# ReLU-squared attention and mixture of depths on one core: heads in a ring of five units instead of three batches

## The chip, the core and the metric

The kernel runs on one core of a Trainium2 chip. The time is that of one execution on the device, in microseconds (us). The core has five instruction queues that run side by side and wait for one another by semaphores: PE (TensorE, matmuls; its weight loads are shown as PEld), ACT (ScalarE), DVE (VectorE), POOL (GpSimd) and SP (SyncE). POOL and SP compute next to nothing here: they start DMAs.

## The reference

Two steps, cut to what is computed. B is 8, H is 12, S is 448, D of a head is 64; the rows of x have 768 elements, F is 1024, and 128 rows of each batch are chosen.

```python
scores = scale * np.matmul(q, k.transpose(0, 1, 3, 2))
attn = np.maximum(scores, 0.0) ** 2 / S
attn_out = np.matmul(attn, v)
x = attn_out.transpose(0, 2, 1, 3).reshape(B, S, H * D)
...
scores = np.einsum('bsd,d->bs', x, w_gate)
out = x.copy()
for b in range(B):
    top_idx = np.argpartition(-scores[b], capacity)[:capacity]
    xe = x[b, top_idx]
    h = np.maximum(xe @ w1, 0.0)
    ye = h @ w2
    g = 1.0 / (1.0 + np.exp(-scores[b, top_idx]))
    out[b, top_idx] = x[b, top_idx] + g[:, None] * ye
```

All inputs and the output are float32 in HBM; on the chip heads, weights and rows are bfloat16, and POOL's DMAs convert while they load.

## The kernel before

**Units.** Four heads make a unit: a batch has NU = 3 units, the kernel 24, numbered u = 3 b + i. A batch of the output ("row" in the words of the change) is 448 rows of x.

**The order is written out.** The string ORDER is a list of some 1200 items; a loop at the end of the kernel calls one function for each, in this order, and nothing reorders them later. Each engine thus gets its own instructions in the order of the list and works through them one after the other; where the data of one comes from another engine, it waits there. The functions, with u a unit, c one of seven chunks of 64 keys, b a batch:

- `L,n,b,i0,i1` (L94) starts on POOL the load of one unit of q, k or v: 224 KB as bfloat16, v in three DMAs. `W` loads a piece of w1 or w2 (256 or 192 KB), 14 in all. The program gives POOL's DMAs eight semaphores in turn, so that a DMA isn't started before the one eight places ahead of it has landed.
- `T,u,n,at` transposes a unit's q or k on PE: 28 matmuls of 64x64 and as many weight loads, 56 instructions. `TE` copies both out of PSUM to qkt on DVE (L185).
- `S,u,c,at`: scores of one chunk, four matmuls of 448 columns (L220). `R,u,c,eng`: ReLU of the scores out of PSUM to r_sb, on ACT (A, L181) or DVE (D, L183). There are 168 S and 168 R, and R is a handy counter of how far the list is: "at R 28" is behind 28 R. `Q,u,c0,c1`: square of four or three chunks in place on DVE (L232).
- `V,u,c,n`: squares times v, four matmuls (L242). `X`: the result, scaled, to xT_sb (L181 or L187), which holds x transposed.
- `XR,u,at` and `XE,u,eng`: x back to rows by eight transposing matmuls on PE (L262) and a copy by ACT or DVE. `XB,u`: the same by two transposing DMAs from SP (L280). Units 0 to 8 (rows 0 to 2) go by XR and XE, 9 to 23 by XB.
- `ST,b,j` stores a quarter of the rows from POOL (L286).
- The second step, for a batch b: `g`, `bc`, `col`, `colE` make the scores of the gate in rows and columns; `rk` (DVE, L330), `cs`, `rank` and `hot` rank them and make a selection matrix; `sel`, `sE` make the indices; `xe`, `xeE` gather by matmul; `h` and `hE`, `y` and `yE` are the two layers; `gs`, `sig` the gate; `ADD` adds the result onto the stored rows by an indirect DMA from POOL (L468). The last batch has forms of its own (`xeh`, `hq`, `yq`, `xs`, `yS`), whose ADD writes whole rows. In the list these stand among the items of later units.

**Buffers.** PSUM is four places of two banks, "pair0" to "pair3", named by the argument `at`; every matmul result goes to one of them, and a place is free again when its result has been read. The heads lie in three buffers for each of q, k and v, one for a batch of three units (NBUF, L61); batch b uses buffer b % 3. qt_pool (transposed heads) and r_pool (scores and squares) have three buffers each, a buffer for a unit.

**The start.** q and k of unit 0 come by SP into float32 staging tiles (`Z,l`) and are converted by ACT and DVE (`Z,q0` to `Z,k1`); the identity for transposes is made by DVE and POOL (`Z,i`), and POOL's constants by `Z,t`, `Zi`.

Of the kernel before, what the change touches and what calls it, by code (L numbers as in the profile page):

```python
# [20 lines left out]
def kernel(  # L21
# [170 lines left out]
    def T(u, n, at):  # L192
# [3 lines left out]
        s_ = sb[n][b % NBUF]  # L196
        for jj in range(NC):
            c = CJ[jj] if n == "q" else jj
            o = S * "qk".index(n) + jj * 64
            for w in range(2):  # L200
                for g in range(2):
                    rows = slice(64 * g, 64 * g + 64)
                    nc.tensor.matmul(  # L203
                        out=t_ps[u][64 * w:64 * w + 64, g, o:o + 64],
                        lhsT=s_[rows, 2 * i + w, c * Dh:c * Dh + Dh], rhs=ident[rows, rows],
                        is_transpose=True, start=(jj == 0 and n == "q"), stop=(jj == NC - 1),
                        skip_group_check=True)
# [272 lines left out]
    R,1,5,A Zi,1 Q,0,4,7,D S,2,2,1 S,2,3,0 L,q,2,2,4 R,2,2,A S,3,0,2 L,k,4,0,2 R,2,3,A Q,1,0,4,D S,2,0,1 V,0,4,3  # L480
    W,2,7 V,0,5,4 V,0,6,5 R,2,0,A V,0,0,6 S,3,2,0 L,v,1,0,2 X,0,A S,3,3,1 R,3,2,D R,3,3,A S,3,5,3 L,q,1,4,6 Zt,0
    V,1,1,0,0 R,3,0,A Q,1,4,7,D V,1,2,1 V,1,3,2 Zi,2 S,3,4,1 L,k,2,2,4 R,3,5,A S,3,1,2 L,q,3,4,6 R,3,4,D R,3,1,A
    V,1,4,3 S,2,1,3 V,1,5,4 L,k,3,0,2 V,1,6,5 R,2,1,A V,1,0,6 Q,3,0,4,D T,4,q,2 S,2,4,1 L,q,3,2,4 T,4,k,2 X,1,A
    S,2,5,3 R,2,4,A L,v,0,4,6 S,2,6,0 TE,4,b,D R,2,6,A S,3,6,1 Q,2,0,4,D R,2,5,A S,4,5,2 L,q,2,0,2 S,4,4,0 R,3,6,A
    L,k,3,2,4 T,5,q,3 T,5,k,3 R,4,4,A S,4,2,1 TE,5,b,D W,1,5 R,4,2,A V,3,1,0,0 V,3,2,1 Q,3,4,7,D V,3,3,2 L,q,4,4,6
    S,4,6,3 R,4,5,A T,7,q,1 T,7,k,1 R,4,6,A W,1,4 S,4,1,2 Q,2,4,7,D V,3,4,3 V,3,5,4 R,4,1,A V,3,6,5 V,3,0,6
    S,4,0,3 L,v,1,2,4 X,3,A V,2,1,0,2 Q,4,4,7,D V,2,2,1 V,2,3,2 V,2,4,3 R,4,0,A V,2,5,4 S,4,3,0 V,2,6,5 L,q,3,0,2
    V,2,0,6 R,4,3,A TE,7,b,D S,5,4,3 L,k,2,4,6 R,5,4,A T,6,q,0 Q,4,0,4,D S,5,5,1 T,6,k,0 X,2,A L,q,4,0,2 S,5,1,3
    R,5,5,A S,5,3,2 L,k,5,2,4 Zt,1 R,5,1,A TE,6,b,D S,5,0,1 Zi,3 R,5,0,A S,5,6,3 W,1,1 R,5,3,D S,6,3,0 R,5,6,A
# [10 lines left out]
    rk,1,1 V,7,3,2 S,8,5,2 TE,10,b,D V,7,4,3 V,7,5,4 R,8,5,A V,7,6,5 V,7,0,6 L,q,5,2,4 sel,0,1 rk,1,2 X,7,A  # L500
    S,10,0,3 S,10,3,2 sE,0,0 Q,8,0,4,D ST,0,2 xe,0,0 xe,0,4 R,10,0,A xe,0,5 xe,0,2 xe,0,3 R,10,3,A XR,7,0
    L,q,5,0,2 xe,0,1 sE,0,1 XR,6,3 XE,7,D xeE,0,2,A W,2,2 T,11,q,2 XE,6,D S,9,0,0 T,11,k,2 S,10,5,1 R,9,0,A rk,1,0
    ST,1,3 h,0,0,3 h,0,2 TE,11,b,D R,10,5,A h,0,1 gs,0,0 L,v,3,0,2 h,0,5 sig,0 Q,8,4,7,D S,9,5,2 S,10,6,0 S,10,4,1
    R,9,5,A h,0,6 h,0,3 L,k,6,4,6 R,10,4,A rk,1,3 h,0,7 cs,1,2 ST,1,2 h,0,4 R,10,6,A rank,1 hot,1 S,9,2,2
    V,8,1,0,1 ST,0,3 V,8,2,1 hE,0,2,D R,9,2,A V,8,3,2 S,9,4,0 V,8,4,3 V,8,5,4 V,8,6,5 R,9,4,A ST,1,0 V,8,0,6
    Q,10,4,7,D S,10,2,2 L,q,6,2,4 y,0,0,0,3 y,0,1,0 X,8,A y,0,0,1 y,0,1,1 y,0,0,3 y,0,1,3 R,10,2,A sel,1,0
    L,v,3,4,6 y,0,0,4 y,0,1,4 Q,9,4,7,D XR,8,1 y,0,0,7 y,0,1,7 XE,8,A y,0,0,5 y,0,1,5 y,0,0,6 y,0,1,6 sE,1,0
    sE,1,1 Q,9,0,4,D L,k,5,0,2 xe,1,4 y,0,0,2 y,0,1,2 xe,1,1 ST,2,1 yE,0,2,A xe,1,5 xe,1,2 L,q,4,2,4 xe,1,0 xe,1,3
    T,12,q,3 xeE,1,2,A L,k,4,2,4 S,11,3,1 T,12,k,3 V,9,1,0,2 R,11,3,A V,9,2,1 TE,12,b,D V,9,3,2 L,q,7,0,2 S,10,1,0
# [110 lines left out]
```

## Time and profile before

| | |
|---|---|
| median of 3 runs | 223.0 us (221.33 to 227.87) |
| profiled execution | 221.9 us |
| its span, first to last instruction | 220.0 us |
| PE, DVE, ACT, POOL busy | 179.7, 171.0, 164.9, 114.2 us |
| HBM read, written | 39.32 MB, 14.16 MB |

The profile is of one execution. A row of the groups has the line, the engine, the operation, result and operands with their shapes, the count; then busy time in us, mean ns of one, and behind the second bar the idle time of the engine in front of them with what ended it. In the table of waits a row says who waited for whom: us in total, times, longest. "issue" is time in which an engine waited for nothing that the profile shows. In the timeline a row has start and length in us, and in brackets the idle time ahead of it. A busy PE isn't a PE at its peak: matmuls are pipelined and their ends are modelled. Busy times of one instruction reach over the start of the next, so the sum of means is above the busy time.

### The profile page before, as it was taken

The page shows a single profiled execution, that of the slowest core. Times are in us where ns is not written, and L with a number is a line of the kernel's source. Part 1 is how long each engine was busy: PE and PEld are TensorE (multiplying, and loading weights), DVE is VectorE, ACT ScalarE, POOL GpSimd, SP SyncE. Part 2 cuts the span into 40 slices and gives each one's busy share as a digit, 9 for nine tenths or more (in the row PEclk, how much of TensorE's full clock was granted, in tenths as well). Part 3 has the DMA queues.
Part 4 walks back from the last instruction along what each step waited for, and adds up shares of the span by engine and source line. Part 5 has one row for each costly group of instructions (what it writes and reads, how often), then busy time and mean ns, then how long its engine had stood idle before and what let it go on. Part 6 is the DMA issues. An engine that isn't in the chain of part 4 may idle for free. (4 is left out here: it accounts for less than half of the span.)

```text
span 220.0 us, 8241 instructions
## 1 busy us (share of the span) xinstructions
PE 179.7 (82%) x3689; PEld 117.9 (54%) x3689; DVE 171.0 (78%) x235; ACT 164.9 (75%) x210; POOL 114.2 (52%) x192
## 2 busy tenths in 40 slices
...
GB/s 182 136 179 145 197 200 204 201 203 199 205 235 216 240 292 202 176 242 239 122 179 166 201 231 191 322 176 114 108 153 221 5 48 51 277 153 106 234 98 0
DMA packets 42383, 38.75 MB, mean 176 GB/s; under 512 B 19110, under 2 KB 38572, under 8 KB 42348
## 3 DMA queue, kind: packets, MB, share of 16 engines
q0 software_dynamic: 25472, 33.37, 83.8%
q1 hardware_dynamic: 16876, 4.86, 18.3%
q8 instruction: 29, 0.48, 0.9%
...
HBM read 39.32 MB, written 14.16 MB: 243 GB/s over the span
## 5 line engine op out<-in xcount | busy, mean ns | idle before, releaser
L181 ACT ACTIVATE r_sb<-s_ps 128x896 bf16<-128x896 f32 x146 | 125.3, 937 | 15.8 <-PE s_ps L220 15.5
L232 DVE TENSOR_TENSOR r_sb<-r_sb 128x3584 bf16<-128x3584 bf16 (+1 forms) x48 | 84.9, 1783 | 3.1 <-ACT r_sb L181 2.7
L220 PE MATMUL s_ps<-qkt 64*64 64x448 bf16 x672 | 60.5, 379 | 14.0 <-ACT r_sb L181 5.2
L242 PE MATMUL o_ps<-r_sb,v_sb 64*64 64x448 bf16 x672 | 46.2, 371 | 4.0 <-issue 3.0
L220 PEld LDWEIGHTS <-qkt 64*64 64x64 bf16 x672 | 23.5, 109 | 34.2 <-issue 25.9
L286 POOL DMA_DIRECT2D out_dram<-x_sb x32 | 18.4, 636 | 45.1 <-DMA x_sb<-xT_sb 35.9
L242 PEld LDWEIGHTS <-v_sb 64*64 64x64 bf16 x672 | 23.0, 112 | 15.7 <-issue 6.6
L102 POOL DMA_DIRECT2D v_sb<-in_v_dram x48 | 28.2, 659 | 6.1 <-DMA k_sb<-in_k_dram 2.9
L183 DVE TENSOR_SCALAR r_sb<-s_ps 128x896 bf16<-128x896 f32 x22 | 23.8, 1087 | 7.8 <-PE s_ps L220 7.1
L185 DVE COPY qkt<-t_ps 128x1792 bf16<-128x1792 bf16 x24 | 25.9, 1084 | 3.3 <-PE t_ps L203 3.3
L291 PE MATMUL y_ps<-w_sb,hT 128*128 128x384 bf16 x128 | 25.6, 327 | 0.5 <-ACT g__4297 L375 0.5
L291 PE MATMUL h_ps<-xeT,w_sb 128*128 128x128 bf16 x384 | 25.5, 222 | 0.2 <-ACT xeT L181 0.2
L468 POOL DMA_INDIRECT out_dram<-gye,idx x8 | 14.3, 1783 | 20.6 <-ACT gye L181 6.6
L291 PEld LDWEIGHTS <-w_sb 128*128 128x128 bf16 x384 | 22.2, 99 | 4.7 <-issue 4.3
L181 ACT ACTIVATE xT_sb<-o_ps 128x896 bf16<-128x896 f32 (+1 forms) x20 | 18.3, 917 | 6.6 <-PE s_ps L220 3.7
...
L100 POOL DMA_DIRECT2D v_sb<-in_v_dram x24 | 16.4, 685 | 4.0 <-DMA k_sb<-in_k_dram 3.6
L203 PE MATMUL t_ps<-ident,q_sb 64*64 64x64 bf16 x672 | 10.6, 198 | 8.9 <-POOL ident L127 5.3
L291 PEld LDWEIGHTS <-hT 128*128 128x128 bf16 x128 | 10.6, 97 | 8.6 <-issue 2.6
L203 PEld LDWEIGHTS <-q_sb 64*64 64x64 bf16 x672 | 9.2, 111 | 11.0 <-ACT q_sb L181 4.8
L330 DVE SCALAR_TENSOR_TENSOR mask<-bc_sb,cols,tie 128x320 bf16<-128x320 f32 (+3 forms) x32 | 14.1, 481 | 0.3
...
## 6 DMA issues: line engine op xcount, KB each, us to landing
...
```

What stands on the lines that cost most here:

```text
L97: nc.gpsimd.dma_start(out=t[:, i0:i1], in_=head_src(n, b, i0, i1))
L100: nc.gpsimd.dma_start(out=t[:, i0:i1:2], in_=s_[:, 0::2])
L102: nc.gpsimd.dma_start(out=t[64 * h:64 * h + 64, i0 + 1:i1:2], in_=s_[64 - 64 * h:128 - 64 * h, 1::2])
L181: nc.scalar.activation(out=out_, in_=in_, func=func or AF.Copy, scale=scale)
L183: nc.vector.tensor_scalar(out=out_, in0=in_, scalar1=0.0, scalar2=None, op0=ALU.max)
L185: nc.vector.tensor_copy(out=out_, in_=in_)
L203: nc.tensor.matmul(out=t_ps[u][64 * w:64 * w + 64, g, o:o + 64], lhsT=s_[rows, 2 * i + w, c * Dh:c * Dh + Dh], rhs=ident[rows, rows], is_t ...
L220: nc.tensor.matmul(out=s_ps[u, c][64 * (g ^ w):64 * (g ^ w) + 64, w, :S], lhsT=qkt[u][rows, g, S + c * 64:S + c * 64 + 64], rhs=qkt[u][row ...
L232: (nc.gpsimd if eng == "P" else nc.vector).tensor_tensor(out=a, in0=a, in1=a, op=ALU.mult)
L242: nc.tensor.matmul(out=o_[64 * g:64 * g + 64, w, :S], lhsT=sb["v"][b % NBUF][rows, 2 * i + w, c * Dh:c * Dh + Dh], rhs=r_sb[u][rows, c, w, ...
L286: nc.gpsimd.dma_start(out=out[b].rearrange("(p c) d -> p c d", c=NC)[:, 4 * g + k0:4 * g + k0 + n], in_=x_rows[b][64 * g:64 * g + 64, k0:k ...
L291: nc.tensor.matmul(out=out_, lhsT=lhsT, rhs=rhs, start=start, stop=stop, skip_group_check=True, **kw)
```

## The change

The heads lie in a ring of NR = 5 buffers for each of q, k and v, one for a unit: unit u uses buffer u % 5. So a load of unit u writes what T (q, k) or V (v) of unit u - 5 has read, and the program waits for that. qt_pool and r_pool get a fourth buffer. Units 9 to 14 (rows 3 and 4) go by XR and XE instead of XB. The list is a new one: the same work in another order, with some evacuations moved between ACT and DVE (R 142 on ACT and 26 on DVE instead of 146 and 22; X 22 and 3 instead of 20 and 5, XE 6 and 9 instead of 2 and 7).

```diff
-    qt_pool = ctx.enter_context(tc.tile_pool(name="qt", bufs=3))
-    r_pool = ctx.enter_context(tc.tile_pool(name="r", bufs=3))
+    qt_pool = ctx.enter_context(tc.tile_pool(name="qt", bufs=4))
+    r_pool = ctx.enter_context(tc.tile_pool(name="r", bufs=4))
...
-    NBUF = 3
-    sb = {n: [const.tile([128, HH, NC * Dh], BF16, name=f"{n}_sb{i}") for i in range(NBUF)]
+    NR = 5
+    sb = {n: [const.tile([128, 2, NC * Dh], BF16, name=f"{n}_sb{i}") for i in range(NR)]
           for n in "qkv"}
...
     def L(n, b, i0, i1):
-        t = sb[n][b % NBUF]
+        t = sb[n][(b * NU + i0 // 2) % NR]
+        s_ = head_src(n, b, i0, i1)
         if n != "v":
-            nc.gpsimd.dma_start(out=t[:, i0:i1], in_=head_src(n, b, i0, i1))
+            nc.gpsimd.dma_start(out=t, in_=s_)
             return
-        s_ = head_src(n, b, i0, i1)
-        nc.gpsimd.dma_start(out=t[:, i0:i1:2], in_=s_[:, 0::2])
+        nc.gpsimd.dma_start(out=t[:, 0], in_=s_[:, 0])
         for h in range(2):
-            nc.gpsimd.dma_start(out=t[64 * h:64 * h + 64, i0 + 1:i1:2],
-                                in_=s_[64 - 64 * h:128 - 64 * h, 1::2])
+            nc.gpsimd.dma_start(out=t[64 * h:64 * h + 64, 1],
+                                in_=s_[64 - 64 * h:128 - 64 * h, 1])
...
-        s_ = sb[n][b % NBUF]
+        s_ = sb[n][u % NR]
...
-                        lhsT=s_[rows, 2 * i + w, c * Dh:c * Dh + Dh], rhs=ident[rows, rows],
+                        lhsT=s_[rows, w, c * Dh:c * Dh + Dh], rhs=ident[rows, rows],
...
-                                 lhsT=sb["v"][b % NBUF][rows, 2 * i + w, c * Dh:c * Dh + Dh],
+                                 lhsT=sb["v"][u % NR][rows, w, c * Dh:c * Dh + Dh],
...
     ORDER = """
-    Z,l Z,f Z,x Z,t L,q,0,2,4 Z,q0 Z,q1 Z,s Z,i L,k,0,2,4 T,0,q,0 Z,k0 Z,k1 L,k,0,4,6 Z,w T,0,k,0 Zg,1 L,k,1,0,2
+    Z,l Z,f Z,x L,q,0,2,4 L,k,0,2,4 L,q,0,4,6 Z,t Z,q0 Z,q1 Zi,0 Z,s Z,i Zt,0 Zi,1 Z,k0 Z,k1 T,0,q,0 Zi,2 Z,w Zt,1
```

The list as the engines get it is seen at three places. First SP, from its first load to its last transposing DMA, before:

```order
L123 DMA qf_100<-in_q_dram 128x2x448
L123 DMA kf_101<-in_k_dram 128x2x448
L124 DMA wgr_102<-in_moe_w_gate_dram 6x128
L280 DMA_TRANSPOSE x_sb_2178<-xT_sb0_94 128x4x128 x6
L280 DMA_TRANSPOSE x_sb_2853<-xT_sb1_95 128x4x128 x6
L280 DMA_TRANSPOSE x_sb_3461<-xT_sb2_96 128x4x128 x6
L280 DMA_TRANSPOSE x_sb_3978<-xT_sb0_94 128x4x128 x6
L280 DMA_TRANSPOSE x_sb_4512<-xT_sb1_95 128x4x128 x6
```

and after:

```order
L123 DMA qf_106<-in_q_dram 128x2x448
L123 DMA kf_107<-in_k_dram 128x2x448
L124 DMA wgr_108<-in_moe_w_gate_dram 6x128
L280 DMA_TRANSPOSE x_sb_3440<-xT_sb2_102 128x4x128 x6
L280 DMA_TRANSPOSE x_sb_4022<-xT_sb0_100 128x4x128 x6
L280 DMA_TRANSPOSE x_sb_4591<-xT_sb1_101 128x4x128 x6
```

The twelve transposing DMAs of rows 3 and 4 are gone; those of rows 5 to 7 stay.

Second DVE, where heads of unit 16 leave PSUM (in the numbers of before qkt_3008 is unit 17 and qkt_3122 unit 16, after qkt_3033 is unit 16); rank and hot are those of batch 3. Before:

```order
L185 COPY qkt_3008<-t_ps_2927 128x1792
L346 TENSOR_TENSOR rank__2879<-cs_ps_3057,rows_2878 128x4
L349 TENSOR_TENSOR hot__2876<-slot_row_112,rank__2879 128x512
L185 COPY qkt_3122<-t_ps_3027 128x1792
L364 COPY sel__2880<-xe_ps_3132 128x2
L232 TENSOR_TENSOR r_sb_2833<-r_sb_2833 128x3584
```

and after:

```order
L185 COPY qkt_3033<-t_ps_2906 128x1792
L346 TENSOR_TENSOR rank__2815<-cs_ps_3025,rows_2814 128x4
L349 TENSOR_TENSOR hot__2812<-slot_row_118,rank__2815 128x512
L183 TENSOR_SCALAR r_sb_2980<-s_ps_3051 128x896
L185 COPY x_sb_2848<-xr_ps_3081 128x4x256
L364 COPY sel__2816<-xe_ps_3096 128x2
L232 TENSOR_TENSOR r_sb_2980<-r_sb_2980 128x3584
```

Before, two units' transposed heads are copied with two small steps between; after, the second of them (unit 17) follows 15 instructions later, and a copy of x by DVE (XE of unit 14) stands between. Over the list T (its q) of units 12 to 18 stands before at R 76, 89, 87, 93, 110, 109, 114 and after at R 83, 88, 93, 98, 105, 115, 119; units 5 and 6 at 28 and 36 before, at 27 and 26 after; 20, 21 and 22 at 136, 140, 144 before and at 124, 130, 143 after.

Third POOL, the loads up to those of unit 5 (before q_sb1 at the end is q of unit 5; after q_sb0 and k_sb0 are q and k of unit 5, in the place that unit 0 had). Before:

```order
L97 DMA k_sb2_90<-in_k_dram 128x2x448
L97 DMA q_sb1_86<-in_q_dram 128x2x448
L158 IOTA tie_i_513 128x320
L97 DMA q_sb2_87<-in_q_dram 128x2x448
L97 DMA k_sb1_89<-in_k_dram 128x2x448
L113 DMA w2_sb_108<-in_moe_w2_dram 128x768
L100 DMA v_sb1_92<-in_v_dram 128x448
L102 DMA v_sb1_92<-in_v_dram 64x448 x2
L97 DMA q_sb1_86<-in_q_dram 128x2x448
```

and after:

```order
L113 DMA w2_sb_114<-in_moe_w2_dram 128x768
L98 DMA k_sb1_91<-in_k_dram 128x2x448
L98 DMA q_sb4_89<-in_q_dram 128x2x448
L113 DMA w2_sb_114<-in_moe_w2_dram 128x768
L98 DMA q_sb1_86<-in_q_dram 128x2x448
L100 DMA v_sb3_98<-in_v_dram 128x448
L102 DMA v_sb3_98<-in_v_dram 64x448 x2
L158 IOTA tie_i_548 128x64
L108 DMA w1_sb_113<-in_moe_w1_dram 128x1024
L98 DMA q_sb2_87<-in_q_dram 128x2x448
L98 DMA q_sb0_85<-in_q_dram 128x2x448
L98 DMA k_sb0_90<-in_k_dram 128x2x448
```

Three weights now stand ahead of the heads of unit 5, where one stood; in the list before, k of unit 5 was the tenth load of all. Before, k of unit 12 was the fifteenth load; after, it is the 44th.

More of the change, by code (lines that the diff above doesn't have):

```diff
@@ L480 @@
[L480 to L489, printed above, removed]
@@ L500 @@
[L500 to L509, printed above, removed]
@@ L565 @@
[L565 to L567 removed]
+    Z,l Z,f Z,x L,q,0,2,4 L,k,0,2,4 L,q,0,4,6 Z,t Z,q0 Z,q1 Zi,0 Z,s Z,i Zt,0 Zi,1 Z,k0 Z,k1 T,0,q,0 Zi,2 Z,w Zt,1
+    T,0,k,0 L,v,0,0,2 Zt,2 Zg,1 TE,0,b,D T,1,q,2 Zw S,0,2,0 L,k,0,4,6 S,0,6,3 R,0,2,A T,1,k,2 R,0,6,D L,k,1,2,4
@@ new lines @@
+    hot,1 L,q,5,2,4 S,10,5,3 V,9,3,2 V,9,4,3 R,10,5,A TE,11,b,D V,9,5,4 L,k,5,2,4 V,9,6,5 V,9,0,6 sel,1,1 X,9,A
+    S,10,4,3 ADD,0 sE,1,0 sE,1,1 S,11,3,0 R,10,4,D xe,1,5 xe,1,1 R,11,3,A XR,9,2 xe,1,4 Q,10,4,7,D XE,9,A xe,1,3
+    xe,1,0 S,10,2,0 L,v,4,4,6 S,10,0,3 R,10,2,A xe,1,2 g,2,0,0,4,2 R,10,0,D xeE,1,2,A XR,8,0 L,v,3,2,4 S,10,1,3
+    XE,8,D S,11,6,1 R,10,1,A g,2,4,4,6 h,1,0,0 h,1,6 bc,2,A Q,10,0,4,D ST,2,1 S,11,0,3 R,11,6,A h,1,2 col,2
+    R,11,0,A h,1,7 gs,1,1 h,1,3 ST,2,3 sig,1 h,1,5 colE,2 rk,2,2 rk,2,3 S,11,2,2 rk,2,0 S,11,4,1 S,11,5,3 R,11,2,A
@@ new lines @@
+    L,k,6,0,2 R,12,2,A TE,13,b,D S,12,3,3 V,11,3,2 V,11,4,3 ADD,1 V,11,5,4 R,12,3,A V,11,6,5 V,11,0,6 sel,2,0
+    S,13,5,1 X,11,A sE,2,0 Q,12,0,4,D S,13,0,3 xe,2,0 xe,2,5 L,v,5,2,4 R,13,0,A xe,2,4 xe,2,1 xe,2,3 xe,2,2
+    R,13,5,A S,12,5,3 xeE,2,2,D T,14,k,2 R,12,5,A L,q,6,0,2 T,14,q,2 S,13,6,1 sE,2,1 S,13,3,0 TE,14,b,D L,k,6,2,4
+    R,13,6,A h,2,0,3 h,2,7 L,q,6,2,4 h,2,5 R,13,3,A Q,12,4,7,D h,2,6 S,14,0,2 S,13,4,1 S,14,5,0 R,14,0,A h,2,2
+    R,13,4,D h,2,4 R,14,5,A h,2,1 h,2,3 Q,13,4,7,D XR,10,1 hE,2,2,A XR,11,0 T,15,q,2 XE,10,A T,15,k,2 XE,11,D
@@ new lines @@
+    S,15,2,0 T,16,q,3 V,13,1,0,2 L,k,7,0,2 V,13,2,1 R,15,2,A V,13,3,2 S,15,0,1 V,13,4,3 Q,14,4,7,D L,q,7,0,2
+    V,13,5,4 V,13,6,5 R,15,0,A V,14,1,0,0 V,13,0,6 ADD,2 V,14,2,1 V,14,3,2 X,13,A cs,3,1 TE,16,b,D V,14,4,3
+    V,14,5,4 V,14,6,5 V,14,0,6 S,15,3,2 L,v,6,0,2 rank,3 hot,3 X,14,A S,15,1,3 g,4,0,0,4,1 R,15,3,D R,15,1,A
+    XR,14,0 g,4,4,4,6 L,v,6,2,4 XE,14,D sel,3,3 XR,13,2 bc,4,A sE,3,0 Q,15,0,4,D S,15,4,0 XE,13,A xe,3,4 xe,3,5
+    xe,3,1 xe,3,3 R,15,4,A xe,3,0 xe,3,2 ST,4,3 col,4 sE,3,1 xeE,3,2,A S,15,5,0 ST,4,1 colE,4 rk,4,0 S,15,6,2
@@ new lines @@
+    Q,16,0,4,D S,17,1,3 R,17,3,A S,17,2,0 L,q,7,4,6 y,3,0,6 y,3,1,6 y,3,0,7 y,3,1,7 R,17,2,A gs,3,1 y,3,0,4
+    y,3,1,4 y,3,0,3 y,3,1,3 R,17,1,D sig,3 T,20,k,0 yE,3,2,A T,20,q,0 S,17,4,1 TE,20,b,D S,17,5,3 R,17,4,A cs,4,2
+    ADD,3 R,17,5,A rank,4 hot,4 S,20,5,0 S,18,6,2 V,16,1,0,1 Q,17,0,4,D V,16,2,1 R,18,6,A V,16,3,2 S,18,3,3
+    V,16,4,3 V,16,5,4 R,18,3,A V,16,6,5 V,16,0,6 sel,4,2 R,20,5,A S,20,3,3 L,v,7,0,2 sE,4,0 X,16,D xe,4,4 xe,4,2
+    R,20,3,A xe,4,1 xe,4,0 sE,4,1 xe,4,3 Q,17,4,7,D xe,4,5 XB,16 T,21,q,3 xeE,4,2,A S,18,4,1 V,17,1,0,0 T,21,k,3
```

144 lines of the change are left out of this document (72 added, 72 removed).

## The prediction

> **What bounds the kernel now.** I read the page first: busy shares, the slices, the DMA queues.
>
> ```profile
> span 220.0 us, 8241 instructions
> PE 179.7 (82%) x3689; PEld 117.9 (54%) x3689; DVE 171.0 (78%) x235; ACT 164.9 (75%) x210; POOL 114.2 (52%) x192
> GB/s 182 136 179 145 197 200 204 201 203 199 205 235 216 240 292 202 176 242 239 122 179 166 201 231 191 322 176 114 108 153 221 5 48 51 277 153 106 234 98 0
> q0 software_dynamic: 25472, 33.37, 83.8%
> q1 hardware_dynamic: 16876, 4.86, 18.3%
> q8 instruction: 29, 0.48, 0.9%
> ```
>
> Three engines are busy for about four fifths each, none for all of it. The profiled execution took 221.9 us (span 220.0 and 1.9 around it), 0.5% under the median of 223.0 of the runs shown; my sum goes from 221.9. Next the table by stretches of 10 us, to see where the fifth is lost:
>
> ```profile
> 20.00:30.00 10.00, 7.08 (x156) 3.75 (x155) 9.28 (x9) 10.00 (x14) 6.74 (x12) 1.00 1.21 189
> 50.00:60.00 10.00, 8.97 (x174) 5.75 (x173) 9.96 (x17) 10.00 (x14) 7.18 (x13) 1.00 1.18 202
> 110.00:120.00 10.00, 8.54 (x110) 5.09 (x110) 6.20 (x5) 5.03 (x6) 3.23 (x6) 0.83 1.29 168
> 170.00:180.00 10.00, 7.18 (x93) 4.61 (x91) 6.42 (x6) 6.22 (x8) 0.00 (x0) 0.83 0.09 19
> ```
>
> Columns are PE, PEld, DVE, ACT, POOL, granted clock, DMA share (over 1 where packets overlap), GB/s. In the first two DVE and ACT are full: both carry the attention (ACT takes scores out, DVE squares). In the last two everything is half empty. So the span is DVE and ACT work plus a few holes. The table of waits names the holes:
>
> ```profile
> ACT r_sb L181 <- PE s_ps L220: 15.5, 20, 2.6
> PE s_ps L220 <- issue: 5.0, 2, 2.8
> PE o_ps L242 <- issue: 3.0, 2, 1.9
> PE t_ps L203 <- issue: 1.0, 1, 1.0
> PE s_ps L220 <- ACT r_sb L181: 5.2, 16, 0.5
> PEld L203 <- DMA q_sb<-in_q_dram: 3.1, 3, 1.5
> PEld L242 <- DMA v_sb<-in_v_dram: 1.7, 4, 1.1
> POOL out_dram L286 <- DMA x_sb<-xT_sb: 35.9, 3, 23.7
> ...
> 186.60 2.10 POOL L286 DMA_DIRECT2D out_dram<-x_sb  x4 [23.75 <-DMA x_sb<-xT_sb]
> ```
>
> ACT waits for scores, and PE, which makes them, waits 5.0 + 3.0 + 1.0 = 9.0 us in five places for "issue": nothing that the profile shows, so no data. POOL's 35.9 us look large, but 23.7 of them are one wait, ended at 186.6, behind which only stores stand in POOL's list. What PE's five places have in common is seen around the first and the last:
>
> ```profile
> 31.35 0.41 PE L203 MATMUL t_ps<-ident,q_sb 64*64 64x64 bf16 x28 [1.17 <-ACT r_sb L181]
> 33.42 0.41 PE L203 MATMUL t_ps<-ident,q_sb 64*64 64x64 bf16 x26
> 33.66 0.42 PE L203 MATMUL t_ps<-ident,k_sb 64*64 64x64 bf16 x27
> 37.53 0.38 PE L242 MATMUL o_ps<-r_sb,v_sb 64*64 64x448 bf16 x2 [1.89 <-issue]
> ...
> 173.08 0.78 PE L220 MATMUL s_ps<-qkt 64*64 64x448 bf16 x8 [2.82 <-issue]
> ...
> q1 hardware_dynamic: 601, 0.14, 48.3%
> q8 instruction: 1, 0.02, 2.5%
> ```
>
> The last two are the DMA queues in 168 to 173 us. The page's 29 instruction packets hold 0.48 MB, one per 2 x 3689 / 29 = 254 of PE's instructions. One packet of 2.5% of 16 engines over 5 us took 2.0 us there, beside transposing DMAs (queue q1) with 48.3%; the mean over the page is 0.9% x 16 x 220 / 29 = 1.1 us. And T of two units is 4 x 28 pairs, 224 instructions, which PE ran through within 2.7 us from 31.35. My reading: PE runs out of fetched instructions where it meets many short ones at once, or where the fetch is slowed. The Trainium skill, "Runtime: NRT & Kernel Launch", section "Instruction fetch mechanics", has blocks of 256 instructions, which fits, but calls the cost of crossing one mostly hidden, which these rows contradict if my reading holds; the rival "no fetch" below is worked out for that case.
>
> **What such a hole costs.** Windows around the middle and the last one, and two shorter waits of ACT:
>
> ```profile
> 107.00:111.00 4.00, 1.80 (x31) 1.12 (x28) 2.62 (x2) 2.55 (x4) 0.46 (x1) 1.00 1.30 143
> 111.00:116.00 5.00, 5.00 (x64) 3.21 (x61) 2.56 (x2) 2.25 (x3) 2.06 (x5) 0.66 1.50 174
> 169.00:173.00 4.00, 1.26 (x22) 1.11 (x19) 1.67 (x2) 2.46 (x3) 0.00 (x0) 1.00 0.48 50
> 173.00:177.00 4.00, 3.92 (x48) 2.64 (x51) 2.75 (x3) 1.84 (x2) 0.00 (x0) 0.57 0.02 4
> 103.71 1.73 ACT L181 ACTIVATE r_sb<-s_ps 128x896 bf16<-128x896 f32 x2 [1.28 <-PE s_ps L220]
> 138.80 0.92 ACT L181 ACTIVATE xT_sb<-o_ps 128x896 bf16<-128x896 f32 x1 [1.31 <-PE s_ps L220]
> ...
> 104.53 5.72 SPq L280 DMA_TRANSPOSE x_sb<-xT_sb  x1
> ```
>
> Behind both long holes the clock is down (0.66, 0.57), so ACT stands idle for 9.0 - 4.8 = 4.2 us around the middle one and 8.0 - 4.3 = 3.7 around the last, more than PE's wait. The Trainium skill ("TensorE: Matmul & The Clock Gate", Part 1) puts the drop to half clock after idle windows of about 3.4 us; here waits of 2.2 and 2.8 us were enough. By that page a shorter hole would cost itself alone, and the sum below would be 218 instead of 216.
>
> **The change part by part.**
>
> *Rows 3 and 4 by TensorE.* Six units leave the transposing DMA for XR on PE and XE; the new order also deals the evacuations anew.
>
> ```profile
> L181 ACT ACTIVATE r_sb<-s_ps 128x896 bf16<-128x896 f32 x146 | 125.3, 937 | 15.8 <-PE s_ps L220 15.5
> L183 DVE TENSOR_SCALAR r_sb<-s_ps 128x896 bf16<-128x896 f32 x22 | 23.8, 1087 | 7.8 <-PE s_ps L220 7.1 <-PE o_ps L242 0.8
> L185 DVE COPY x_sb<-xr_ps 128x1024 bf16<-128x1024 bf16 x7 | 4.7, 684 | 0.0
> L181 ACT ACTIVATE x_sb<-xr_ps 128x1024 bf16<-128x1024 bf16 x2 | 2.1, 1028 | 0.3 <-PE xr_ps L262 0.3
> L187 DVE TENSOR_SCALAR xT_sb<-o_ps 128x896 bf16<-128x896 f32 x4 | 4.4, 1088 | 3.2 <-PE o_ps L242 3.2
> L262 PE MATMUL xr_ps<-ident,xT_sb 128*128 128x128 bf16 x72 | 5.2, 219 | 0.6 <-DVE qkt L185 0.3 <-ACT r_sb L181 0.2
> L291 PE MATMUL h_ps<-xeT,w_sb 128*128 128x128 bf16 x384 | 25.5, 222 | 0.2 <-ACT xeT L181 0.2
> ```
>
> ACT: four XE more, 4 x 1.03 = +4.1; four R fewer, 4 x 125.3/146 = -3.4; two X more, about +1.8: +2.5. DVE: two XE more, 2 x 0.68 = +1.4; four R more, 4 x 1.09 = +4.3; two X fewer, -2.2: +3.5. The single swaps of hE, yE, xeE and bc between the two cancel within 1 us. Each of the two gets about 3 us; PE gets 48 matmuls at 5.2/72, 3.5 us. Where DVE and ACT are full this costs its 3, where the holes are it costs nothing; rows 3 and 4 lie in the middle of the order, partly in holes: **+2.0**, bounds 0 and +3.5.
>
> What leaves is 6/15 of queue q1, 7% of the DMA time of the span. Nobody waits for it directly except POOL's stores; what I expect from it is in the next term.
>
> *The new order and the ring.* In the order before, units 14 and 13 are transposed with two R between them, 17 and 16 with one, 18 four R behind. After, 12 to 18 come 5, 5, 5, 7, 10 and 4 R apart; one tight pair (6 and 5) stays. From unit 15 on loads are issued within 5 R of the ring freeing their place, 24 to 46 R ahead of their use, so a late load has cover. Of the five holes I count out those in the middle: the one ahead of 103.71 and the one from 108 us (a transposing DMA of row 3 runs at 104.53, units 13 to 15 are transposed) and the one ahead of 138.80 (units 16 to 18). They cost ACT 1.28 + 4.2 + 1.31 = 6.8 us. Bounds: 0, if as many holes open elsewhere; all five and their dips gone, 6.8 + 3.7 + about 2 for the first = 12.5. I take **-6.8**, since what made the first and last hole is still there: a tight pair early, and rows 5 to 7 by DMA.
>
> *Fourth buffers.* With four r_sb a unit's scores may be taken out while three older ones are squared and multiplied. No row shows a wait for a free r_sb, since the order is fixed around it; what they can relieve is the rest of ACT's 15.5 us of waiting for scores, less some 9 in the holes: 0 to -6. Nearest are PE's waits for ACT's places, 5.2 in 16 pieces of at most 0.5, which extra SBUF buffers don't end: **-1.5**.
>
> *Loads at the start.* Three loads are now issued ahead of POOL's constants instead of one, but the staged q and k gate the first scores in any case: 0. Until about 60 us the DMA is full (1.21 and 1.18 above), and 640 KB of weights now stand ahead of unit 5's k, none before. By the GB/s row (slices of 5.5 us) the first five slices moved 4.61 MB, 0.92 of it the staged q and k; the new order's first 19 loads end with this k and are 4.33 MB, so it lands at 27.5 + 0.63/0.200 = 30.6 us. The old order transposed unit 5 at 33.42 us, at R 28, where the new one asks for this k: 2.8 us of cover. 0; without the cover 640 KB at 189 GB/s, +3.4.
>
> *The tail.* Two more h steps stand behind the last V, 2 x 25.5/64 = 0.8, in front of hE of batch 6; part of it beside the ranking of batch 7: **+0.6**. POOL's four stores of batch 7 now stand before ADD of batch 6: 0, as DVE's last gye ends the chain.
>
> Sum: 221.9 + 2.0 - 6.8 - 1.5 + 0.6 = 216.2; **216** us.
>
> **The rivals.**
>
> *No fetch.* PE's waits have another cause, or open as often in the new order. Then 221.9 + 2.0 + 0.6 - 1.5 = 223. For it: the hole at 173 us had no crowd of transposes before it. Against: it had a slowed packet.
>
> *All holes close.* 216 - 5.7 = 210. For it: no two units' transposes stand close in the second half but 17, 18 and 20. Against: rows 5 to 7 keep their transposing DMAs, and the pair 6 and 5 is as tight as before.
>
> *More holes (slower).* The new order packs PE's list at another place: units 17, 18 and 20 are transposed within nine R, 3 x 112 = 336 short instructions, soon after XR of units 10 to 14 (16 instructions each). If fetching fails there twice and nowhere less, two long holes at the measured 4.2 and 3.7 come on top: 223 + 7.9 = 231. Up to five holes it is 223, with six 227: it decides from the sixth. For it: units 16 to 18 within five R did open a hole before. Against: no transposing DMA of rows 3 and 4 runs near it any more.
>
> *The ring doesn't pace.* If POOL stays limited by the DMA everywhere, the loads move as before and nothing follows from the ring; this lies within "no fetch".
>
> **How the numbers follow.** Forecast 216: 0.45 (own range 212 to 220); all holes close, 210: 0.15; no fetch, 223: 0.29; more holes, 227 to 231: 0.11. The range from 208 to 225 leaves out most of the last case and a little of the others. A change of 2% is what a measurement here tells from none; from 223.0 that is 218.5 and 227.5. Faster: 0.15 + 0.40 + 0.02 = 0.57; slower: 0.10; same: 0.33.
>
> **What would show it.** Right: PE's waits for issue at 4 us or less, none between 100 and 140 us, fewer windows at half clock; queue q1 near 11% of the DMA time. The busy time of ACT and DVE up by about 3 us each. Wrong: the same waits for issue at other places; PE waiting for k of unit 5 at about 31 us; DVE busy as now and ACT waiting for scores as long without any hole, which would mean the order alone sets the pace.

## The result and the profile after

The changed kernel takes 210.1 us (median of four runs, 209.6 to 211.2), the kernel before 222.2 us on the same chip (220.3 to 227.9). The ratio is 0.949, with a 95% interval from 0.940 to 0.958. The execution that was profiled took 209.6 us. Some runs of most kernels below are disturbed and take over 1.5% longer than the fastest of the same kernel; the ratios leave these out, and so do times that are listed one by one.

First the page of the changed kernel: span, busy times, the granted clock in 40 slices, and the queue of the transposing DMAs.

```profile
span 207.8 us, 8344 instructions
...
PE 177.1 (85%) x3737; PEld 116.2 (56%) x3737; DVE 174.0 (84%) x239; ACT 167.7 (81%) x212; POOL 114.6 (55%) x192
...
PEclk9999999999999999999999999999999999999995
...
q1 hardware_dynamic: 10348, 3.28, 11.9%
```

DVE has 3.0 us more work than before and ACT 2.8, in a span that is 12.2 us shorter: the time came out of their idle time. PE has 2.6 us less, though it got 48 matmuls more; the granted clock was 0.987 on the mean, against 0.964 before, and no slice but the last is at a lower one. Two of the stretches of 10 us that were half empty before:

```profile
110.00:120.00 10.00, 9.99 (x197) 6.01 (x197) 9.86 (x18) 8.43 (x12) 6.61 (x10) 1.00 1.02 211
...
170.00:180.00 10.00, 9.90 (x151) 5.97 (x151) 9.72 (x18) 9.72 (x14) 4.73 (x5) 1.00 0.43 69
```

PE, PEld, DVE, ACT, POOL, clock, DMA share and GB/s again: DVE went from 6.2 to 9.9 us in the first and from 6.4 to 9.7 in the second. From the table of waits after (total, times, longest):

```profile
ACT r_sb L181 <- PE s_ps L220: 11.2, 17, 4.0
...
DVE r_sb L183 <- PE s_ps L220: 2.6, 4, 1.4
...
ACT hT L181 <- PE h_ps L291: 1.7, 3, 0.8
...
DVE xT_sb L187 <- PE o_ps L242: 1.2, 1, 1.2
...
DVE qkt L185 <- PE t_ps L203: 1.2, 3, 0.5
...
PE t_ps L203 <- issue: 1.0, 2, 0.7
...
PE s_ps L220 <- issue: 0.3, 1, 0.3
```

And four rows of the same table before, which the prediction's sum did not add up by themselves:

```profile
DVE r_sb L183 <- PE s_ps L220: 7.1, 8, 2.9
...
ACT hT L181 <- PE h_ps L291: 4.4, 3, 3.1
...
DVE xT_sb L187 <- PE o_ps L242: 4.3, 4, 2.3
...
DVE qkt L185 <- PE t_ps L203: 3.3, 4, 1.2
```

PE's waits for issue fell from 9.0 us in five places to 1.3 in three. ACT's wait for scores fell by 4.3 us only. But these four smaller rows of ACT and DVE fell by 4.5, 2.7, 3.1 and 2.1 us. They alone don't show a gain apart from the five holes: the longest wait of each row before ended at 173.5, 113.1, 116.1 and 139.3 us, 0.4 to 5.3 us behind the end of a hole (173.1, 110.7, 110.7 and 137.8). So a hole seems to be paid by DVE too, and in more rows of ACT than the one for scores.

The tail did not move. The last scores taken out, first of the kernel before, then of the changed one:

```profile
188.37 4.26 ACT L181 ACTIVATE r_sb<-s_ps 128x896 bf16<-128x896 f32 x5
```

```profile
178.21 1.77 ACT L181 ACTIVATE r_sb<-s_ps 128x896 bf16<-128x896 f32 x2
```

From there to the end of the span it is 220.0 - 192.6 = 27.4 us before and 207.8 - 180.0 = 27.8 us after. All that was gained lies ahead of that point.

### The profile page after: what moved, and what is told of

Same layout as the page of the kernel before. It is cut to its first block, busy times and chain, and to the rows that moved or that the text cites. A ratio compares the mean times of both kernels' runs of the same rounds, so it can differ in the third digit from the quotient of the medians.

```text
span 207.8 us, 8344 instructions
## 1 busy us (share of the span) xinstructions
PE 177.1 (85%) x3737; PEld 116.2 (56%) x3737; DVE 174.0 (84%) x239; ACT 167.7 (81%) x212; POOL 114.6 (55%) x192
## 3 DMA queue, kind: packets, MB, share of 16 engines
q1 hardware_dynamic: 10348, 3.28, 11.9%
## 5 line engine op out<-in xcount | busy, mean ns | idle before, releaser
L181 ACT ACTIVATE r_sb<-s_ps 128x896 bf16<-128x896 f32 x142 | 122.3, 939 | 11.7 <-PE s_ps L220 11.2
L220 PE MATMUL s_ps<-qkt 64*64 64x448 bf16 x672 | 55.9, 371 | 6.7 <-ACT r_sb L181 4.4
L242 PE MATMUL o_ps<-r_sb,v_sb 64*64 64x448 bf16 x672 | 42.6, 351 | 0.9 <-ACT r_sb L181 0.7
L220 PEld LDWEIGHTS <-qkt 64*64 64x64 bf16 x672 | 21.4, 106 | 24.8 <-issue 16.9
L183 DVE TENSOR_SCALAR r_sb<-s_ps 128x896 bf16<-128x896 f32 x26 | 28.1, 1085 | 2.7 <-PE s_ps L220 2.6
L286 POOL DMA_DIRECT2D out_dram<-x_sb x32 | 17.7, 614 | 22.1 <-DMA x_sb<-xT_sb 15.1
L102 POOL DMA_DIRECT2D v_sb<-in_v_dram x48 | 28.5, 665 | 1.0 <-DMA k_sb<-in_k_dram 0.6
L242 PEld LDWEIGHTS <-v_sb 64*64 64x64 bf16 x672 | 20.5, 106 | 9.7 <-issue 2.5
L181 ACT ACTIVATE xT_sb<-o_ps 128x896 bf16<-128x896 f32 (+1 forms) x22 | 20.6, 935 | 3.0 <-PE o_ps L242 2.9
L100 POOL DMA_DIRECT2D v_sb<-in_v_dram x24 | 16.8, 700 | 7.4 <-PE s_ps L220 2.9
L203 PEld LDWEIGHTS <-q_sb 64*64 64x64 bf16 x672 | 9.8, 113 | 12.2 <-ACT q_sb L181 4.6
L330 DVE SCALAR_TENSOR_TENSOR mask<-bc_sb,cols,tie 128x64 bf16<-128x64 f32 (+3 forms) x32 | 14.0, 481 | 0.3
```

The lines of the kernel that those rows point to most:

```text
L100: nc.gpsimd.dma_start(out=t[:, 0], in_=s_[:, 0])
L102: nc.gpsimd.dma_start(out=t[64 * h:64 * h + 64, 1], in_=s_[64 - 64 * h:128 - 64 * h, 1])
L181: nc.scalar.activation(out=out_, in_=in_, func=func or AF.Copy, scale=scale)
L183: nc.vector.tensor_scalar(out=out_, in0=in_, scalar1=0.0, scalar2=None, op0=ALU.max)
L203: nc.tensor.matmul(out=t_ps[u][64 * w:64 * w + 64, g, o:o + 64], lhsT=s_[rows, w, c * Dh:c * Dh + Dh], rhs=ident[rows, rows], is_transpose ...
L220: nc.tensor.matmul(out=s_ps[u, c][64 * (g ^ w):64 * (g ^ w) + 64, w, :S], lhsT=qkt[u][rows, g, S + c * 64:S + c * 64 + 64], rhs=qkt[u][row ...
```

## The experiments

My theory after the result: the transposing DMAs of rows 3 and 4 delayed the fetch of PE's instructions, so taking them away closed the holes, and the new order closed the rest. The rivals: the order alone did it, by keeping PE's short instructions apart; or the ring did, by pacing the loads; or the holes have nothing to do with fetching. The kernel before had medians of 220.8 to 222.7 us beside the several sets; ratios are to the one of the same set. Where there is no ratio, single times stand in its place.

**The parts of the change, one at a time.** Three kernels. The first is the kernel before with units 9 to 14 turned by TensorE (e3_before_rows_by_PE); the second is the changed kernel with these units turned by DMA again (e2_after_rows_by_DMA); the third has the old order of the computing steps in the new ring, with fourth buffers, and the loads of q, k and v in the changed kernel's sequence (e4_before_order_in_ring). Of these, 16 stand up to 7 R later than in the changed kernel, and the 14 loads of w1 and w2 stay where the kernel before has them.

```diff
 e3, in the ORDER of before; units 9 to 14
-XB,9
+XR,9,1 XE,9,A
 e2, in the ORDER of after; units 9 to 14
-XR,9,2 XE,9,A
+XB,9
 e4, before with the order of its computing steps kept
-bufs=3 (qt, r)   NBUF = 3, a place per batch
+bufs=4           NR = 5, a place per unit, loads of q, k, v in the sequence of after
```

> The kernel before, but units 9 to 14 turned by XR and XE. If the transposing DMAs opened the holes of the middle: the two at 101 and 108 us close, 215 to 219 us. If they did not: the holes stay and the added work costs 0 to 3.5 us, 222 to 226 us.

> The changed kernel, but units 9 to 14 turned by transposing DMAs again (XB in the place of XE, XR left out). If the transposing DMAs slowed the fetches and so opened the holes of the middle: holes and a dip are back there and the time is 213 to 217 us. If the order closed them: 207 to 210 us, since ACT and DVE are spared about 3 us each.

> The order of before on all engines but POOL's loads, with the changed kernel's ring of five, its fourth buffers and the order and places of its loads. If ring, buffers and pacing bring the gain: 213 us or less. If the order of TensorE's work does: 219 to 225 us and the same holes of issue as before.

Measured, as ratios to the kernel before: e3 0.981 (0.972 to 0.989), 217.0 us; e2 0.978 (0.965 to 0.991), 217.4 us; e4 1.048 (1.036 to 1.061), 231.7 us. So rows 3 and 4 by TensorE are worth about 5 us in the old order and 7 in the new one, and the rest of the change about 5 with these rows by DMA and 7 without. The two halves add up to the 12, within what the intervals can tell. The ring, the buffers and the new sequence of loads cost 9 us in the old order, which lies above both ranges that were expected of e4; e2 lies 0.4 us above the range for DMAs that slow the fetch, and e3 in it.

In e2 the holes are back, here two of PE's rows:

```profile
89.97 0.25 PE L203 MATMUL t_ps<-ident,q_sb 64*64 64x64 bf16 x6 [2.05 <-issue]
...
110.65 0.24 PE L203 MATMUL t_ps<-ident,k_sb 64*64 64x64 bf16 x5 [1.97 <-issue]
```

In e3, without those DMAs but with the old order, the middle holes are gone, and of the five that before had only the first and the last are left above 0.6 us.

What the holes have in common shows when PE's instructions are counted along its list. The five holes of before stand at positions 1,217, 3,777, 4,033, 5,057 and 6,337, all multiples of 256 apart, and those of over 1 us in e2, e3 and e5 stand in the same row of numbers (within one). An instruction packet of 16 KB moves for each step of 256, 29 in all, and every one of these holes ends 1.3 to 1.5 us after such a packet has landed. Over the kernel before, a packet begins 2.5 us (median) after PE has begun on the 256 ahead of it; the packet of the hole that ended at 110.7 us began 6.2 us after. So PE has run through its 256 before the next have come.

**Transposing or only DMA?** e2 also takes instructions out of PE's list, which moves everything behind them. So two kernels leave the changed kernel whole and add twelve transfers of 128 KB behind the XE of units 9 to 14, into a tile that nobody reads: transposing ones (e5_after_extra_transposes), or plain copies of the same bytes on the same queue (e6_after_extra_copies).

```diff
+    def XD(u):                                  # e5; in e6 dma_start
+        for w in range(2):
+            nc.sync.dma_start_transpose(out=xd[u % 2, w], in_=xT_sb[b % NX][:, 2 * i + w, :])
-... XE,9,A
+... XE,9,A XD,9
```

> The changed kernel with nothing taken out: units 9 to 14 are still turned by TensorE, and behind each XE two transposing DMAs copy the same rows once more into a scratch tile that nobody reads. No engine's list of instructions changes but SP's. If transposing DMAs slow the fetch of PE's instructions (and the loads), the waits that the changed kernel lost come back although the order and the count of PE's instructions are those of the changed kernel: 214 to 218 us, PE waits of 1 to 2 us for issue between 85 and 160 us. If what counted in the run with rows 3 and 4 by DMA was the place of PE's block borders or the late rows themselves, it stays at 209 to 212 us.

> As the run with extra transposing DMAs, but the twelve extra transfers are plain copies of the same 128 rows of 512 values, same queue, same places, not transposing. If any DMA traffic of this size slows the fetch, the same time as that run (214 to 218 us). If it is the transposing alone, 209 to 212 us, with no wait of PE for issue over 1 us.

e5 took 215.9 and 218.7 us, e6 210.3 and 211.4, the changed kernel 209.6 to 211.2; the profiled spans are 216.9 and 209.6, against 207.8 of the changed kernel. The same place of PE's list, first in e5 (with PE's waits for issue in all), then in e6:

```profile
121.33 0.90 PE L220 MATMUL s_ps<-qkt 64*64 64x448 bf16 x5 [4.65 <-issue]
...
PE s_ps L220 <- issue: 4.7, 1, 4.7
...
PE t_ps L203 <- issue: 2.7, 3, 1.5
```

```profile
118.44 0.54 PE L220 MATMUL s_ps<-qkt 64*64 64x448 bf16 x5 [0.88 <-issue]
```

PE's list is the same in both, so neither the order nor the number of instructions makes the difference. Nor do late loads: PE waits 3.0 us for q, k and v in e5 and 3.4 in the changed kernel, but 7.4 us for issue against 1.3. The queues of e5 from 111 to 118 us, and then from 118 to 121:

```profile
q0 software_dynamic: 524, 1.05, 81.8%
q1 hardware_dynamic: 1069, 0.26, 62.6%
```

```profile
q0 software_dynamic: 429, 0.81, 108.9%
q8 instruction: 1, 0.02, 2.2%
```

In the first window no instruction packet moved at all, while the transposing queue held 62.6% of the DMA time. The packet itself is short, 2.2% of 16 engines over 3 us, 1.1 us. It came late, and PE went on 1.4 us after it had landed. It began 6.7 us after PE had begun on the 256 instructions ahead of it, and in e6, at the same place of the list, 2.9 us after. When it was asked for is not in the trace.

What the extra transfers took, in e5 and then in e6: the queue over the whole execution (packets, MB, share of the DMA time), and ten of the twelve transfers in the view from 80 to 160 us (the last number is the median us from issue to landing).

```profile
q1 hardware_dynamic: 16876, 4.86, 18.3%
...
xd<-xT_sb SPq DMA_TRANSPOSE x10, 11.3
```

```profile
q1 hardware_dynamic: 12076, 4.86, 13.6%
...
xd<-xT_sb SPq DMA_DIRECT2D x10, 128.0 KB, 6.3
```

In the changed kernel this queue holds 11.9% of 207.8 us, 24.7 us of the time of all 16 DMA engines. The same extra bytes add 15.0 us to that when they are transposed (18.3% of 216.9) and 3.8 as copies (13.6% of 209.6), in 6,528 packets against 1,728. The spans are 9.1 and 1.8 us longer; the spans of the changed kernel's own four runs differ by 1.5, so the copies may cost nothing. Whether the transposing itself hurts, the many small packets or only the DMA time stays open. The Trainium skill ("Advanced Engine Details and Errata", section "X-Bar Transpose (TRN2)") has transposing DMAs as fast as regular ones; for these pieces from SBUF to SBUF the trace does not agree, 11.3 us against 6.3.

**Fewer instructions.** T does its transposes in 14 matmuls over 128 rows in place of 28 over 64, which shortens PE's list by 1,344 instructions (e1_before_half_T, on the kernel before).

```diff
-            for w in range(2):
-                for g in range(2):
-                    rows = slice(64 * g, 64 * g + 64)
-                    ... lhsT=s_[rows, ...], rhs=ident[rows, rows] ...
+            for w in range(2):
+                ... lhsT=s_[:, ...], rhs=ident ...
```

> The kernel before, same order and buffers, but each transposing step T takes 14 matmuls over all 128 rows in place of 28 over 64, so that TensorE's list is 1,344 instructions shorter (7,378 to 6,034). If the holes are instruction fetches that come too late: TensorE's waits for issue fall from 9.0 us to 3 or less, the dips of the clock go, and the time is 209 to 214 us. If the holes have another cause, or the order alone made the gain: waits for issue as before and 219 to 225 us.

It took 221.4 us (216.8 to 226.3), and even the fastest run lies above the expected 209 to 214. PE's waits for issue are gone from its table, but PE is busy 8.4 us more, and near the place where the kernel before had its middle hole, PE now waits for a load:

```profile
115.52 0.57 PE L242 MATMUL o_ps<-r_sb,v_sb 64*64 64x448 bf16 x1 [3.00 <-DMA v_sb<-in_v_dram]
```

So the holes can go and the time stay. Which of the two takes the gain back, PE's added work or late loads beside the transposing DMAs (29.4% of the DMA time from 100 to 112 us), this run does not tell.

**Moved borders.** If PE's instructions come in blocks of 256, some 112 pairs more at the start move the borders of all blocks by 224 and the holes with them. Matmuls of zeros, before any data is there, went into e3's kernel (e7_before_rows_PE_shifted) and into the changed one (e10_after_shifted).

```diff
+    def Zd(n, at):
+        for i in range(n):
+            nc.tensor.matmul(out=d_ps, lhsT=dum, rhs=dum, start=(i == 0), stop=(i == n - 1))
-    Z,l Z,f Z,x ...
+    Z,l Z,f Zd,112,3 Z,x ...
```

> The kernel before with rows 3 and 4 by TensorE (217.0 us), and 112 matmuls of zeros (224 instructions of PE) at its start, which only move the borders of the blocks of 256 instructions to places where PE runs no block through in less than 4.9 us. Theory of the fetch: the first wait (at 37.5 us) and the last (169.7 us) close, PE has no wait for issue over 1 us. If the new order is worth only what those two waits cost, the time comes to 209 to 213 us; if the order has a worth of its own, it stays at 213 to 216. If the waits have nothing to do with blocks, they stay where they are, and the time with them: 217 to 219 us.

> The changed kernel with the same 112 matmuls of zeros at its start as the old order had in the shifted run (217.8 us profiled, no wait of PE at a block border). They move its block borders by 224 instructions and end PE's start by up to 1 or 2 us later. If the changed order is free of waits only because its borders lie well, waits of 1 to 2 us for issue return: 213 to 217 us. If the borders hardly matter with few transposing DMAs, 210 to 213; then the old order without waits and the new one stand 5 to 7 us apart for another reason than fetching.

The same steps of the list in e3 and then in e7:

```profile
167.03 0.38 PE L220 MATMUL s_ps<-qkt 64*64 64x448 bf16 x4
169.71 0.49 PE L291 MATMUL h_ps<-xeT,w_sb 128*128 128x128 bf16 x6 [2.30 <-issue]
```

```profile
167.24 0.38 PE L228 MATMUL s_ps<-qkt 64*64 64x448 bf16 x4
167.55 0.51 PE L299 MATMUL h_ps<-xeT,w_sb 128*128 128x128 bf16 x6
```

The hole goes with the border, and so does the first one (37.5 us): the waits are at block borders. But the time does not follow. e7 took 217.0 and 217.8 us, e3 216.4, 216.4 and 217.6. The 3.7 and some 2 us that the prediction put down for these two holes are not there. One thing besides the holes differs: by the clock records of the traces e7 ran at half clock from 31.7, 41.9 and 103.4 us on, 3.4 us each, e3 only from 38.8 (the last 10 us of both left out). That may hide part of a gain. The changed kernel with the same start took 210.2 us, ratio 0.954 (0.943 to 0.966): it is not its borders that make it fast. So two kernels without a hole of over 1 us at a border stand 7 to 8 us apart. Where? The windows from 100 to 140 us, e7, then e10:

```profile
100.00:120.00 20.00, 17.67 (x301) 12.78 (x301) 15.99 (x17) 14.83 (x19) 16.79 (x29) 0.91 1.15 209
120.00:140.00 20.00, 18.45 (x462) 12.89 (x461) 15.74 (x32) 16.38 (x21) 11.43 (x15) 1.00 0.80 157
```

```profile
100.00:120.00 20.00, 19.99 (x391) 13.15 (x389) 19.31 (x26) 17.34 (x23) 15.16 (x23) 1.00 1.15 212
120.00:140.00 20.00, 19.46 (x493) 13.32 (x492) 18.93 (x27) 19.11 (x25) 9.98 (x15) 1.00 1.11 188
```

DVE did 31.7 us of work in these 40 us in the old order and 38.2 in the new one, ACT 31.2 and 36.5. That is 6.5 and 5.2 of the 8.4 us between the spans (216.0 and 207.6). A part is the clock, 0.91 against 1.00 in the first of these windows. What ACT and DVE waited for there in e7, the longest rows of each:

```profile
ACT x_sb L189 <- PE xr_ps L270: 2.9, 3, 1.5
ACT r_sb L189 <- PE s_ps L228: 2.8, 4, 1.5
ACT xeT L189 <- PE xe_ps L299: 1.6, 1, 1.6
```

```profile
DVE x_sb L193 <- PE xr_ps L270: 2.0, 2, 1.3
DVE cols L332 <- ACT r_sb L189: 1.8, 1, 1.8
```

In e10 no wait of ACT or DVE there is longer than 0.8 us. My reading is that in the old order steps such as turning rows or gathering tokens stand in PE's list where nothing else is ready for ACT and DVE, and in the new one something is; no run tests this by itself. Up to 4.9 us of the waits in e7, those for xr_ps, come from how e3 and e7 were made: each XE stands right behind its XR there, and two to five items later in the new order.

**Ring and buffers without the transposing DMAs** (e9_before_rows_PE_in_ring): e4 with units 9 to 14 by TensorE, so all of the change but the new order of the computing steps and of the loads of weights.

```diff
 the kernel of e4; units 9 to 14
-XB,9
+XR,9,1 XE,9,A
```

> The order of before with rows 3 and 4 by TensorE, in the ring of five units with the loads at the changed kernel's places, and four buffers for squares and transposed heads: all of the change but the new order of the computing steps. If the ring and the buffers have a worth of their own once the transposing DMAs are gone, 211 to 214 us (217.0 without them). If they only serve the new order, 216 to 220. If the old order cannot live with loads at these places (its loads then come late, as in the run with rows 3 and 4 by DMA, 231.7), 222 to 228, with PE waiting over 3 us for q or k.

229.9 us, ratio 1.043 (1.032 to 1.054): slow even without those DMAs, and 2 us above the worst that was expected. Its waits between 25 and 65 us, and its window from 30 to 60; behind them the same window of e3:

```profile
POOL k_sb L98 <- PE t_ps L203: 10.6, 2, 9.1
...
PEld L203 <- DMA q_sb<-in_q_dram: 4.0, 1, 4.0
...
PE t_ps L203 <- DMA q_sb<-in_q_dram: 3.6, 1, 3.6
```

```profile
30.00:60.00 30.00, 20.58 (x443) 11.22 (x445) 22.58 (x20) 22.65 (x29) 17.60 (x31) 0.83 0.91 141
```

```profile
30.00:60.00 30.00, 23.70 (x573) 14.18 (x576) 27.52 (x31) 27.62 (x36) 21.04 (x36) 0.94 1.22 204
```

POOL stands 9.1 us before a full place for k, with loads of q behind it in its list; the DMA, full in e3 (204 GB/s), moves 141 GB/s meanwhile, and PE then waits 3.6 us for q. The old order uses units too late for a ring of five that is loaded in the new sequence. It loses 5 us of work on DVE and on ACT in this stretch alone.

**A larger ring** (e11_after_ring_of_six), the changed kernel with places for six units:

```diff
-    NR = 5
+    NR = 6
```

> The changed kernel with places for six units in the ring instead of five: the loads stand at the same places in POOL's list, but POOL's waits for a free place (8.1 us for q, 4.3 for k, 2.9 for v) go, and the loads start earlier. If the pace that the ring gives is worth something, it gets slower: 212 to 215 us. If the ring is only room, it stays at 209 to 211; if the ring is too tight and loads come late, it gets faster, 207 to 209.

212.2 us, ratio 0.964 (0.955 to 0.973). It gains nothing from starting loads earlier. It lies at the lower end of what was expected if the pace is worth something, and PE's waits for issue are 3.6 us instead of 1.3; but that it is slower than with five cannot be told, since the intervals overlap. The ring is room, and its pace is worth little at most.

**Row 5 by TensorE too** (e8_after_row5_by_PE), the changed kernel with units 15 to 17 turned on PE:

```diff
-XB,15   XB,16   XB,17
+XR,15,3 XE,15,D   XR,16,0 XE,16,A   XR,17,0 XE,17,D
```

> The changed kernel with the rows of batch 5 (units 15 to 17) by TensorE too, two evacuations on DVE and one on ACT. If transposing DMAs still cost fetches and loads there, 206 to 209 us; if they are harmless where the changed kernel has them, it costs the three evacuations and 24 matmuls, 210 to 212 us.

213.0 us, ratio 0.962 (0.951 to 0.974): no gain, and 1 us above what was expected if the DMAs are harmless there. From row 5 on the loads have thinned out, and the transposing DMAs that remain seem to hold nobody up.

**The price of a wait** (e12_after_three_waits). Three waits of PE in the changed kernel, each for a transfer of 8 KB:

```diff
+    def ZH(at):                  # before S,6,0  S,10,2  S,13,1
+        matmul(out=h_, lhsT=hole_sb, rhs=hole_sb)
+        nc.sync.dma_start(out=hole_sb, in_=ident[:64, :64])
+        matmul(out=h_, lhsT=hole_sb, rhs=hole_sb)
```

> The changed kernel with three waits put into PE's list, ahead of a score step of unit 6, of unit 10 and of unit 13, near 48, 77 and 104 us: PE may go on only when a transfer of 8 KB, issued on SP's queue when PE gets there, has landed (some 2 to 4 us each, which the trace will show). It prices such a wait by itself, in an order that has none there. If a wait costs what I put down for the long ones of before (4.2 us of ACT for 2.2 us of PE, the half clock behind it included), it comes to 218 to 224 us. If it costs its own length, 216 to 220. If the steps that ACT and DVE have in hand cover it, as the old order without waits at its block borders suggests (no gain from closing two of them), 210 to 214.

The row of these waits, and the window around the third:

```profile
PE hole_ps L171 <- DMA hole_sb<-ident: 16.2, 3, 5.9
```

```profile
120.00:130.00 10.00, 3.30 (x71) 1.99 (x75) 2.10 (x2) 0.92 (x1) 2.50 (x4) 0.66 0.69 125
```

233.9 us (232.0 to 235.7), ratio 1.061 (1.043 to 1.078). The waits came out longer than meant, 5.4 us each, 16.2 in all, and the time went up by 233.9 - 210.1 = 23.8 us, above all that was expected: 1.5 us for each us that PE stands, so on the whole none of it was covered. The clock is down there (0.66 in the window).

## Why the prediction was right, and where it was not

The sign and the range held, and the holes closed: 216 was forecast, within 208 to 225, and 210.1 came. Of the signs that were named, PE's waits for issue are 1.3 us (at most 4 said), with one of 0.66 at 104.5 us, where none was said; the transposing queue has 11.9% (near 11 said), and half clock is left at the end alone. But twice the forecast gain came, outside the 212 to 220 of the forecast's own case; that the range held it owes something to its width. The result is the rival "all holes close", priced at 210, but it is reached by another sum: rows 3 and 4 with the middle holes were put at 2.0 - 6.8 = -4.8 us and came to -5.3 (e3); the rest was put at -1.5 + 0.6 = -0.9 and came to -6.9 (e3 to the changed kernel).

- **Rows 3 and 4, +2.0.** The work came as counted. The groups after:

```profile
L181 ACT ACTIVATE r_sb<-s_ps 128x896 bf16<-128x896 f32 x142 | 122.3, 939 | 11.7 <-PE s_ps L220 11.2
...
L183 DVE TENSOR_SCALAR r_sb<-s_ps 128x896 bf16<-128x896 f32 x26 | 28.1, 1085 | 2.7 <-PE s_ps L220 2.6
...
L181 ACT ACTIVATE x_sb<-xr_ps 128x1024 bf16<-128x1024 bf16 x6 | 6.2, 1026 | 0.2 <-PE xr_ps L262 0.2
```

  ACT's total rose by 2.8 us (2.5 said), DVE's by 3.0 (3.5 said). With what leaves the DMAs, the step is worth -5 to -7 us (e3, e2). I wrote that nobody but POOL's stores waits for the transposing DMAs directly. PE does, by way of its instruction packets (e5); whether loads are late beside them too is not settled (e1).
- **The middle holes, -6.8, put down to the new order.** The size was about right and the agent wrong: the term named crowded transposes and DMAs of row 3, and taking the DMAs away is enough. e3 has the old order and no hole in the middle: 217.0 us, where +2.0 and -6.8 on the 222.3 of the kernel before beside it make 217.5. And e5 has the new order and a hole of 4.65 us. That all of e3's 5 us comes from closed holes, and none from loads that land sooner, is not shown. I had read a packet of 2.0 us, against 1.1 on the mean, as the slow fetch. That was the last hole alone: at the other four of before the packet took 0.9 to 1.0 us, and in e5 1.1. What costs there is that the packet begins late.
- **First and last hole kept.** They closed too; in the changed kernel one wait of 0.66 us is the longest at issue. But in e7 closing these two gained nothing that could be measured.
- **Fourth buffers and the order's own worth, -1.5.** This is the term that was mis-sized. With rows 3 and 4 by TensorE on both sides, the rest of the change gives 7 us (e3 to the changed kernel), with them by DMA 5 (the kernel before to e2). e7 and e10 show that holes at borders don't make it: most of it lies between 100 and 140 us, where ACT and DVE wait for PE's results in waits of at most 1.8 us; some is the clock, and some of the 7 is how e3 was made. I had counted the order for holes only. The buffers and the ring, in the old order, give nothing (e4, e9): they are what the new list needs. It was not tried with three buffers, since the new list asks for a fourth before it has freed the first.
- **Loads at the start, 0.** The k of unit 5 was put at 30.6 us, with 2.8 us of cover. The new order asked for it earlier than I thought:

```profile
30.93 0.41 PE L203 MATMUL t_ps<-ident,k_sb 64*64 64x64 bf16 x28 [0.49 <-DMA k_sb<-in_k_dram]
```

  It landed just ahead of 30.9, and PE waited half a microsecond. The landing was right, the cover was not there. ACT was busy without a break from 28.2 to 33.3 us, so nothing came of it.
- **The tail, +0.6.** 27.4 to 27.8 us: +0.4.
- **What a hole costs.** I had 4.2 us of ACT for 2.2 of PE, 1.9 for one. e12 gives 1.5 for one, on longer waits; e5 gives some 7 us for 6.1 us more of waits, and e7 nothing for two holes of 4.3 us in all. So there is no one price; that it goes by what ACT and DVE have in hand is my guess. The Trainium skill ("TensorE: Matmul & The Clock Gate", Part 1) lets the clock drop after about 3.4 us without work; the traces don't agree: the clock fell 1.1 to 1.8 us into the waits of e12, and behind the 2.2 us of the kernel before.
- **The rival "no fetch"** falls: the holes stand at steps of 256 instructions, go with the borders (e7) and come back with DMAs whose data PE never uses (e5). **"More holes"** did not come: six XR and a crowd of transposes at units 17, 18 and 20 opened none. **"The ring doesn't pace"** is the nearer to the truth of what was said about the ring: six places do no worse than can be told from five, and what the ring does without its order is harm.

So my sum missed by 6 us because it priced a new order by the five conspicuous waits that it could close, and left out the many short ones. That it is these waits, and which items of the new order end them, rests on the comparison of e7 and e10; the cause is narrowed to the order of PE's work, not proved item by item.
